# Low parts of weights, keys and activations: subtraction on VectorE in place of GpSimd

## The chip, the cores and the metric

The kernel runs on one core of a Trainium2 chip. The metric is the device time of one execution in microseconds. The engines are named as in the profile: PE is TensorE's matrix product and PEld its weight load, DVE is VectorE, ACT is ScalarE, POOL is GpSimd, SP issues transfers.

## What is computed

Causal attention by blocks of 64 on 4 batches, 8 heads, 576 positions, head size 64; then a two-layer block with squared ReLU; then a routed layer in which each of the 2304 tokens goes to one of 8 experts:

```python
attn_out = _attn_ref(q, k, v)                  # softmax(q k^T / 8, block-causal) v
x = attn_out.transpose(0, 2, 1, 3).reshape(B * S, H * D)      # 2304 x 512
r = np.maximum(x @ w_in, 0.0)                  # w_in 512 x 2048
x = (r * r) @ w_out                            # w_out 2048 x 512
logits = x @ w_gate + modality_bias[modality_id]
e_idx = np.argmax(logits, axis=1)
out[mask] = gate_w[mask, None] * (np.maximum(x[mask] @ w1[e], 0.0) @ w2[e])
```

## The kernel before

Matrix products run on fp32r operands. To keep precision, an operand is split in a high part, rounded to fp32r, and a low part, the difference; a product is then three products (high by high, high by low, low by high) into one PSUM bank. Names ending in `h` are high parts, those in `l` low parts. The rounding to the high part is a copy on ScalarE (or, for half of the expert weights, VectorE). The low part is one two-input subtraction.

The attention goes by batch, by chunks of 128 query rows (the fifth has 64), and by four pairs of heads (`attn_pair`). Keys are split once per head by `load_k`: L197 copies, L198 subtracts, on 64 of the 128 partitions. A K tile arrives in a raw buffer that is shared with the weights' pool `w`; only few of its buffers are free, so the next K load starts when L198 has read the one before. For the first batch the keys come in two parts, of 256 and 320 columns; for others in one of 576.

The weights of the first block are 64-bit words. `split_weight64` rebuilds a 32-bit float: L147 on ScalarE, three integer instructions on VectorE (L148, L149, L151), a copy on ScalarE (L153), and the subtraction L154. Sixteen pairs of 128x512 tiles are converted this way in the first part of the run, while the first two chunks of attention and the first block of tokens are computed. `split_weight` does the same for the two experts that get most tokens, for 32 tiles: every other tile (L164, L165) by ScalarE and GpSimd, the rest (L167, L168) by VectorE alone.

`ffn_units` computes 256 tokens at a time, in 16 units. A unit makes 12 products into `h` (L397 to L399), then r = relu(h) on ScalarE (L410), r*r (L411), the high part gh on ScalarE (L412), the low part gl (L413); the six products with the second weight (L387 to L389) follow after the next unit's first products. L411 runs on GpSimd in the first token block (`startup`) and on VectorE later. When a block is done, `route` computes the expert of each token and writes pairs to a list in DRAM by two indirect scatters from GpSimd (L494). Later GpSimd gathers rows (L547) and scatters results (L568).

The order on each engine is set by a scheduler that simulates the program while it is built; each engine then runs its instructions strictly in that order, waiting on semaphores. A changed engine for one instruction therefore changes the order of many others.

Of the kernel before, what the change touches and what calls it, by code (L numbers as in the profile page):

```python
# [10 lines left out]
F32 = mybir.dt.float32  # L11
# [9 lines left out]
P = 128  # L21
B, H, S, HD = 4, 8, 576, 64
# [28 lines left out]
def tile_attention_mlp_moe(ctx: ExitStack, tc: tile.TileContext, qT2, kT2, v, w_in, w_out,  # L51
                           mod, wg, bias, w1, w2, out):
    nc = tc.nc
# [9 lines left out]
    def pbank(tag, bufs):  # L63
        return ps.tile([P, 512], F32, tag=tag, bufs=BANKS[tag], name=tag)
# [63 lines left out]
    def wtile(dt):  # L128
        return wpool.tile([P, 2 * 512], dt, tag="w", bufs=2 * NF1 + 1, name="w")

    def parts_of(w):
        return w[:, 0:512], w[:, 512:1024]
# [7 lines left out]
    def split_weight64(raw):  # L140

        wh, wl = parts_of(wtile(F32R))
        wf = apool.tile([P, S], F32, tag="p", bufs=5, name="wf")[:, 0:512]
        wi = wf.bitcast(I32)
        words = raw.rearrange("p (f c) -> p f c", c=2)
        top, low = words[:, :, 1], words[:, :, 0]
        nc.scalar.activation(out=wf, in_=top.bitcast(F32), func=AF.Abs, scale=2.0 ** -112)  # L147
        nc.vector.tensor_scalar(wi, wi, 3, None, op0=ALU.logical_shift_left)  # L148
        nc.vector.scalar_tensor_tensor(out=wi, in0=top, scalar=-0x80000000, in1=wi, op0=ALU.bitwise_and,  # L149
                                       op1=ALU.bitwise_or)  # L150
        nc.vector.scalar_tensor_tensor(out=wi, in0=low, scalar=29, in1=wi, op0=ALU.logical_shift_right,  # L151
                                       op1=ALU.bitwise_or)
        nc.scalar.copy(wh, wf)  # L153
        nc.gpsimd.tensor_sub(wl, wf, wh.bitcast(F32))  # L154
        return wh, wl

    def split_weight(src):
        wh, wl = parts_of(wtile(F32R))
        raw = late.tile([P, 512], F32, tag="wraw", bufs=4, name="wraw")
        dst = raw.rearrange("p (k f) -> p k f", k=src.shape[1]) if len(src.shape) == 3 else raw  # L160
        nc.sync.dma_start(dst, src)
        nsplit[0] += 1
        if nsplit[0] % 2:
            nc.scalar.copy(wh, raw)  # L164
            nc.gpsimd.tensor_sub(wl, raw, wh.bitcast(F32))  # L165
        else:
            nc.vector.tensor_copy(wh, raw)  # L167
            nc.vector.tensor_sub(wl, raw, wh.bitcast(F32))  # L168
        return wh, wl
# [16 lines left out]
    def load_k(b, h, part=None):  # L186

        if part != 1:
            kst[b, h] = apool.tile([P, S], F32R, tag="ks", bufs=8, name=f"ks{b}_{h}")
        ks = kst[b, h]  # L190
        if part is None:
            raw = wtile(F32)[:, 0:S]
            nc.sync.dma_start(raw, kT2[b, h])
        else:
            raw = kpre[h][part]
            ks = (ks[:, 0:KS], ks[:, KS:S])[part]
        nc.scalar.copy(ks, raw)  # L197
        nc.gpsimd.tensor_sub(ks[HD:P], raw[HD:P], ks[HD:P].bitcast(F32))  # L198

    def load_v(b, hp, nk):  # L200
        vt = apool.tile([P, 5, P], F32, tag="v", bufs=2, name="v")
# [11 lines left out]
    startup = [True]  # L213
# [138 lines left out]
    def attn_units():  # L352

        res = []
        for b in range(B):
            for ci, (r0, nr) in enumerate(CHUNKS):
                for hp in range(H // 2):
                    def f(b=b, ci=ci, r0=r0, nr=nr, hp=hp):
                        if b == 0 and ci < 2:
                            load_k(b, 2 * hp, ci)  # L360
                            load_k(b, 2 * hp + 1, ci)
                        attn_pair(b, r0, nr, hp)
                        if ci == len(CHUNKS) - 1 and b < B - 1:
                            load_k(b + 1, 2 * hp)
                            load_k(b + 1, 2 * hp + 1)
                    nk = r0 + nr
                    cost = 2 * 2 * max(nk, 256) + 2 * nk * 3
                    res.append((b * S + r0, cost, f))
        return res


    def ffn_units(xh, xl, wa, wb, nf, square, finish, htag="h", bt=BT, last_blk=False):
        nt = -(-bt // P)
        acc = []
        pend = []

        def mm2(f, gh, gl):
            for t in range(nt):
                if f == 0:
                    acc.append(pbank("acc" if t < 2 else "h", 2))  # L380
                mm2t(f, t, gh, gl)

        def mm2t(f, t, gh, gl):
            wh, wl = wb[f]
            sl = slice(t * P, min((t + 1) * P, bt))
            n = sl.stop - sl.start
            nc.tensor.matmul(acc[t][:n], gh[:, sl], wh, start=(f == 0), stop=False)  # L387
            nc.tensor.matmul(acc[t][:n], gh[:, sl], wl, start=False, stop=False)  # L388
            return nc.tensor.matmul(acc[t][:n], gl[:, sl], wh, start=False, stop=(f == nf - 1))  # L389

        def unit(f):
            hb = pbank(htag, 2)
            wh, wl = wa[f]
            whk = wh.rearrange("p (k f) -> p k f", k=KC)
            wlk = wl.rearrange("p (k f) -> p k f", k=KC)
            for k in range(KC):
                nc.tensor.matmul(hb[:, :bt], whk[:, k, :], xh[:, k, :], start=(k == 0), stop=False)  # L397
                nc.tensor.matmul(hb[:, :bt], whk[:, k, :], xl[:, k, :], start=False, stop=False)  # L398
                nc.tensor.matmul(hb[:, :bt], wlk[:, k, :], xh[:, k, :], start=False, stop=(k == KC - 1))  # L399
            if last_blk:  # L400
                gh, gl = (x[:, :bt] for x in parts_of(wtile(F32R)))
            elif bt == BT:
                gh = work.tile([P, BT], F32R, tag="gh", bufs=3, name="gh")
                gl = work.tile([P, BT], F32R, tag="gl", bufs=3, name="gl")
            else:
                gh = late.tile([P, bt], F32R, tag="lgh", bufs=3, name="gh")
                gl = late.tile([P, bt], F32R, tag="lgl", bufs=3, name="gl")
            if square:
                r = work.tile([P, BT], F32, tag="r", bufs=2, name="r")
                nc.scalar.activation(out=r, in_=hb[:, :bt], func=AF.Relu)  # L410
                (nc.gpsimd if startup[0] else nc.vector).tensor_mul(r, r, r)  # L411
                nc.scalar.copy(gh, r)  # L412
                nc.gpsimd.tensor_sub(gl, r, gh.bitcast(F32))  # L413
            else:
                nc.scalar.activation(out=gh, in_=hb[:, :bt], func=AF.Relu)  # L415
                nc.vector.scalar_tensor_tensor(out=gl, in0=hb[:, :bt], scalar=0.0, in1=gh.bitcast(F32),  # L416
                                               op0=ALU.max, op1=ALU.subtract)
            pend.append((f, gh, gl))
            if len(pend) > 1 and not last_blk:
                mm2(*pend.pop(0))  # L420

        res = [lambda f=f: unit(f) for f in range(nf)]

        def last():
            if last_blk:
                for t in range(nt):
                    acc.append(pbank("acc", 2))
                    with tc.issue_after(mm.ins) if t else ExitStack():
                        for f, gh, gl in pend:
                            mm = mm2t(f, t, gh, gl)  # L430
                    finish(acc, t)
                return
            while pend:
                mm2(*pend.pop(0))
            for t in range(nt):
                finish(acc, t)
        res.append(last)
        return res
# [193 lines left out]
    def conv(f):  # L632
        if len(w_b) <= f < NF1:
            w_a.append(split_weight64(raws[2 * f]))
            w_b.append(split_weight64(raws[2 * f + 1]))
            if f + PRE < NF1:
                load_mlp(f + PRE)
# [21 lines left out]
    def expert_loads(i):  # L659
        wa, wb = [], []  # L660
        moe_w[i] = (wa, wb)

        def load(f):
            r = loads_reg(i)
            wa.append(split_weight(w1[ds(r, 1), :, f * P:(f + 1) * P].rearrange("o (k p) f -> p (o k) f", p=P)))
            wb.append(split_weight(w2[ds(r, 1), f * P:(f + 1) * P, :].rearrange("o p d -> p (o d)")))
        return [lambda f=f: load(f) for f in range(NF2)]
# [96 lines left out]
    with tc.If(njob > 0):  # L764
        with tc.For_i(0, E) as e:
            ne = nc.values_load(meta[0:1, ds(e, 1)], min_val=0, max_val=N // P)
            st = nc.values_load(meta[0:1, ds(e + E, 1)], min_val=0, max_val=CAP)
            with tc.If(ne > 0):
# [4 lines left out]
                with tc.For_i(0, ne) as c:  # L773
# [11 lines left out]
                    gh = gp.tile([P, FE], F32, name="ggh")  # L785
# [45 lines left out]
```

## Time and profile before

| what | value |
|---|---|
| median of three runs | 946.83 us (944.97 to 949.15) |
| profiled execution | 944.93 us |
| its span, first to last instruction | 943.0 us |
| mean granted TensorE clock | 0.975 |
| TensorE busy | 869.1 us (92%) |
| TensorE weight load | 742.4 us (79%) |
| VectorE busy | 516.6 us (55%) |
| ScalarE busy | 391.0 us (41%) |
| GpSimd busy | 314.2 us (33%) |

Shares are means over stages that differ: the attention and weight conversion at the start, the token blocks in the middle, the experts at the end. An instruction's duration in the trace includes the time in which it is held up after its start. Durations of VectorE instructions overlap a little with the next one's start, so what one takes out of the engine's time is the distance from start to start when it is fed without a break. PEclk is the granted share of TensorE's full clock.

### The profile page before, as it was taken

The numbers are of one execution on the slowest core, as the hardware profiler recorded it, in microseconds if no ns is written. First come the engines' busy times: TensorE is split into PE (matmuls) and PEld (weight loads), VectorE is DVE, ScalarE is ACT, GpSimd is POOL, SyncE is SP. The second block draws the span as 40 slices with busy tenths as digits, with TensorE's granted clock in tenths as the row PEclk, the third lists the DMA queues.
The fourth block names the chain that finished last, engine by engine and source line by source line (L and its number), as shares of the span: only waits on it lengthen the run. The fifth ranks groups of instructions, "written<-read, shape, count | busy, mean of one in ns | idle before, by whom it ended". The sixth has DMA issues, their size and how long they took to land. (4 is left out here: it accounts for less than half of the span.)

```text
span 943.0 us, 16448 instructions
## 1 busy us (share of the span) xinstructions
PE 869.1 (92%) x5961; PEld 742.4 (79%) x5962; DVE 516.6 (55%) x1411; ACT 391.0 (41%) x1076; POOL 314.2 (33%) x422
## 2 busy tenths in 40 slices
PE   5488878999989999989999999999898899999997
PEld 3266667788868888878888888888787688888896
DVE  5999997686637766536563664316622722122121
ACT  6566665555435544435443453334321312121111
POOL 3675766321333121234221221234612621021011
PEclk9689989999999999999999999999999999999999
DMA  9991114222133112034111111033303521010000
GB/s 315 286 321 48 48 40 116 79 48 79 53 91 100 60 43 57 26 90 114 49 29 40 41 51 38 26 80 108 84 23 77 187 65 42 20 58 31 12 28 36
DMA packets 87926, 73.98 MB, mean 78 GB/s; under 512 B 14305, under 2 KB 75745, under 8 KB 87842
## 3 DMA queue, kind: packets, MB, share of 16 engines
q1 hardware_dynamic: 84194, 63.18, 22.6%
q0 software_dynamic: 3648, 9.72, 3.3%
q8 instruction: 48, 0.79, 0.4%
q14 instruction: 36, 0.29, 0.1%
HBM read 62.71 MB, written 10.42 MB: 78 GB/s over the span
## 5 line engine op out<-in xcount | busy, mean ns | idle before, releaser
L413 POOL TENSOR_TENSOR gl<-r,gh 128x256 fp32r<-128x256 f32 x144 | 112.1, 779 | 284.9 <-ACT gh L412 197.0
L397 PE MATMUL h<-xh,w 128*128 128x256 f32 x576 | 169.8, 295 | 1.3 <-ACT w L153 1.3
L387 PE MATMUL acc<-w,gh 128*128 128x512 f32 x400 | 164.2, 411 | 3.7 <-ACT gh L412 2.9
L398 PE MATMUL h<-xl,w 128*128 128x256 f32 x576 | 164.8, 286 | 2.3 <-DVE xl L350 2.2
L399 PE MATMUL h<-xh,w 128*128 128x256 f32 x576 | 164.7, 286 | 1.4 <-POOL w L154 1.4
L388 PE MATMUL acc<-w,gh 128*128 128x512 f32 x400 | 158.5, 397 | 0.0
L389 PE MATMUL acc<-w,gl 128*128 128x512 f32 x400 | 143.4, 406 | 10.3 <-POOL gl L413 8.0
L397 PEld LDWEIGHTS h<-xh,w 128*128 128x128 f32 x576 | 110.7, 192 | 10.9 <-issue 3.8
L398 PEld LDWEIGHTS h<-xl,w 128*128 128x128 f32 x576 | 110.7, 192 | 6.5 <-DVE xl L350 2.5
L411 DVE TENSOR_TENSOR r<-r 128x256 f32<-128x256 f32 x128 | 64.3, 502 | 93.6 <-ACT r L410 93.4
L399 PEld LDWEIGHTS h<-xh,w 128*128 128x128 f32 x576 | 110.9, 193 | 2.3 <-POOL w L154 2.0
L410 ACT ACTIVATE r<-h 128x256 f32<-128x256 f32 x144 | 55.7, 386 | 119.7 <-PE h L399 117.3
L389 PEld LDWEIGHTS acc<-w,gl 128*128 128x128 f32 x400 | 72.7, 189 | 29.0 <-POOL gl L413 10.7
L416 DVE SCALAR_TENSOR_TENSOR gl<-pt,gh 128x352 fp32r<-128x352 f32 (+1 forms) x56 | 26.9, 480 | 124.8 <-ACT gh L415 124.8
L387 PEld LDWEIGHTS acc<-w,gh 128*128 128x128 f32 x400 | 76.2, 191 | 15.9 <-ACT gh L412 4.8
L412 ACT CAST gh<-r 128x256 fp32r<-128x256 f32 x144 | 58.5, 406 | 65.3 <-DVE r L411 65.0
L415 ACT ACTIVATE gh<-pt 128x352 fp32r<-128x352 f32 (+1 forms) x56 | 24.1, 430 | 144.2 <-PE pt L399 144.2
L388 PEld LDWEIGHTS acc<-w,gh 128*128 128x128 f32 x400 | 75.9, 190 | 9.2 <-POOL w L154 0.3
L397 PE MATMUL pt<-gxh,w 128*128 128x256 f32 (+1 forms) x256 | 78.5, 307 | 4.7 <-DVE gl L416 4.7
L399 PE MATMUL pt<-gxh,w 128*128 128x256 f32 (+1 forms) x256 | 77.7, 304 | 0.0
L398 PE MATMUL pt<-gxl,w 128*128 128x256 f32 (+1 forms) x256 | 77.6, 303 | 0.0
L286 ACT ACTIVATE p<-s,nmx 128x384 f32<-128x384 f32 (+2 forms) x96 | 56.5, 591 | 37.5 <-DVE nmx L281 17.3
(176 smaller groups left out, 1691.8 us busy)
## 6 DMA issues: line engine op xcount, KB each, us to landing
w<-w_in SPq DMA_DIRECT2D x16, 512.0 KB, 6.9
w<-w_out SPq DMA_DIRECT2D x16, 512.0 KB, 7.6
wraw<-w SPq DMA_DIRECT2D x32, 256.0 KB, 3.0
v<-v SPq DMA_DIRECT2D x28, 256.0 KB, 3.0
w<-kT SPq DMA_DIRECT2D x24, 288.0 KB, 2.9
qraw<-qT SPq DMA_DIRECT2D x48, 128.0 KB, 2.2
x2d<-x SPq DMA_DIRECT2D x18, 256.0 KB, 2.3
v<-v SPq DMA_DIRECT2D x12, 192.0 KB, 2.5
```

The costliest lines, as they stand in the source:

```text
L286: nc.scalar.activation(out=pb[:, c0:c0 + nv], in_=banks[i][:, :nv], func=AF.Exp, bias=nmx[:, 0:1], accum_out=sm[:, i:i + 1])
L387: nc.tensor.matmul(acc[t][:n], gh[:, sl], wh, start=(f == 0), stop=False)
L388: nc.tensor.matmul(acc[t][:n], gh[:, sl], wl, start=False, stop=False)
L389: return nc.tensor.matmul(acc[t][:n], gl[:, sl], wh, start=False, stop=(f == nf - 1))
L397: nc.tensor.matmul(hb[:, :bt], whk[:, k, :], xh[:, k, :], start=(k == 0), stop=False)
L398: nc.tensor.matmul(hb[:, :bt], whk[:, k, :], xl[:, k, :], start=False, stop=False)
L399: nc.tensor.matmul(hb[:, :bt], wlk[:, k, :], xh[:, k, :], start=False, stop=(k == KC - 1))
L410: nc.scalar.activation(out=r, in_=hb[:, :bt], func=AF.Relu)
L411: (nc.gpsimd if startup[0] else nc.vector).tensor_mul(r, r, r)
L412: nc.scalar.copy(gh, r)
L413: nc.gpsimd.tensor_sub(gl, r, gh.bitcast(F32))
L416: nc.vector.scalar_tensor_tensor(out=gl, in0=hb[:, :bt], scalar=0.0, in1=gh.bitcast(F32), op0=ALU.max, op1=ALU.subtract)
```

## The change

Five subtractions go from GpSimd to VectorE: L154 (low part of a first-block weight), L165 (of every other expert weight), L198 (of a key), L413 (of gl), and L411 (the square) in the first token block too. GpSimd keeps memsets, setup and the indirect transfers.

```diff
--- before.py
+++ after.py
@@ -151,7 +151,7 @@
         nc.vector.scalar_tensor_tensor(out=wi, in0=low, scalar=29, in1=wi, op0=ALU.logical_shift_right,
                                        op1=ALU.bitwise_or)
         nc.scalar.copy(wh, wf)
-        nc.gpsimd.tensor_sub(wl, wf, wh.bitcast(F32))
+        nc.vector.tensor_sub(wl, wf, wh.bitcast(F32))
         return wh, wl
 
     def split_weight(src):
@@ -162,7 +162,7 @@
         nsplit[0] += 1
         if nsplit[0] % 2:
             nc.scalar.copy(wh, raw)
-            nc.gpsimd.tensor_sub(wl, raw, wh.bitcast(F32))
+            nc.vector.tensor_sub(wl, raw, wh.bitcast(F32))
         else:
             nc.vector.tensor_copy(wh, raw)
             nc.vector.tensor_sub(wl, raw, wh.bitcast(F32))
@@ -195,7 +195,7 @@
             raw = kpre[h][part]
             ks = (ks[:, 0:KS], ks[:, KS:S])[part]
         nc.scalar.copy(ks, raw)
-        nc.gpsimd.tensor_sub(ks[HD:P], raw[HD:P], ks[HD:P].bitcast(F32))
+        nc.vector.tensor_sub(ks[HD:P], raw[HD:P], ks[HD:P].bitcast(F32))
 
     def load_v(b, hp, nk):
         vt = apool.tile([P, 5, P], F32, tag="v", bufs=2, name="v")
@@ -408,9 +408,9 @@
             if square:
                 r = work.tile([P, BT], F32, tag="r", bufs=2, name="r")
                 nc.scalar.activation(out=r, in_=hb[:, :bt], func=AF.Relu)
-                (nc.gpsimd if startup[0] else nc.vector).tensor_mul(r, r, r)
+                nc.vector.tensor_mul(r, r, r)
                 nc.scalar.copy(gh, r)
-                nc.gpsimd.tensor_sub(gl, r, gh.bitcast(F32))
+                nc.vector.tensor_sub(gl, r, gh.bitcast(F32))
             else:
                 nc.scalar.activation(out=gh, in_=hb[:, :bt], func=AF.Relu)
                 nc.vector.scalar_tensor_tensor(out=gl, in0=hb[:, :bt], scalar=0.0, in1=gh.bitcast(F32),
```

The scheduler's order shows the move at two places. The first is VectorE while weights are converted (wf is a weight being rebuilt, w its split tile, r and gl belong to a unit of the first token block). Before:

```order
L149 SCALAR_TENSOR_TENSOR wf_642<-w_166,wf_642 128x512
L148 TENSOR_SCALAR wf_650<-wf_650 128x512
L151 SCALAR_TENSOR_TENSOR wf_642<-w_166,wf_642 128x512
L149 SCALAR_TENSOR_TENSOR wf_650<-w_168,wf_650 128x512
L292 TENSOR_SCALAR sm_686<-sm_686 128x1
L292 TENSOR_SCALAR sm_704<-sm_704 128x1
L151 SCALAR_TENSOR_TENSOR wf_650<-w_168,wf_650 128x512
L293 RECIPROCAL sm_686<-sm_686 128x1
L293 RECIPROCAL sm_704<-sm_704 128x1
```

Now, at the conversion of the same tile (wf_650):

```order
L154 TENSOR_TENSOR w_578<-wf_579,w_578 128x512
L294 TENSOR_SCALAR p_596<-p_596,sm_595 128x384
L411 TENSOR_TENSOR r_676<-r_676 128x256
L294 TENSOR_SCALAR p_614<-p_614,sm_613 128x384
L149 SCALAR_TENSOR_TENSOR wf_650<-w_168,wf_650 128x512
L151 SCALAR_TENSOR_TENSOR wf_642<-w_166,wf_642 128x512
L292 TENSOR_SCALAR sm_686<-sm_686 128x1
L411 TENSOR_TENSOR r_765<-r_765 128x256
L413 TENSOR_TENSOR gl_675<-r_676,gh_674 128x256
L151 SCALAR_TENSOR_TENSOR wf_650<-w_168,wf_650 128x512
L313 MEMSET s_785 64x64
L292 TENSOR_SCALAR sm_704<-sm_704 128x1
```

Between the integer instructions now stand the subtraction of an earlier tile (w_578), two squares and a gl, which were in GpSimd's queue.

The second place is the change from the second batch to the third, with what each instruction waits for (DMASW is a transfer issued by GpSimd, DMAHW one issued by SP, ks a split key). On GpSimd before:

```order
L494 DMA lst_70<-pay_2925,pos_2944 22528x2 [waits DVE_49,Pool_49]
L413 TENSOR_TENSOR gl_3267<-r_3268,gh_3266 128x256 [waits Activation_49]
L494 DMA lst_70<-pay_2925,pos_2944 22528x2 [waits DMASW2_49]
L198 TENSOR_TENSOR ks2_2_3538<-w_3539,ks2_2_3538 64x576 [waits DMASW3_49,DMAHW7_49,Activation_49,Pool_49]
L413 TENSOR_TENSOR gl_3352<-r_3353,gh_3351 128x256 [waits Activation_49,Pool_49]
L198 TENSOR_TENSOR ks2_3_3543<-w_3544,ks2_3_3543 64x576 [waits DMAHW1_49,Activation_49,Pool_49]
```

On VectorE now, around the same gl_3352 and the same key ks2_2:

```order
L411 TENSOR_TENSOR r_3353<-r_3353 128x256 [waits Activation_49]
L281 TENSOR_REDUCE nmx_3494<-s_3497 128x1 [waits PE_49]
L281 TENSOR_REDUCE nmx_3494<-s_3502 128x1 [waits PE_49]
L247 SCALAR_TENSOR_TENSOR qlo_3724<-qraw_3718,qhi_3725 128x2x64 [waits DMAHW3_49,Activation_49,Pool_49]
L413 TENSOR_TENSOR gl_3352<-r_3353,gh_3351 128x256 [waits Activation_49]
L349 CAST xh3_2130<-pv_2994 128x64 [waits PE_49]
L220 COPY pt_3096<-pt_3097 128x512
L284 TENSOR_TENSOR nmx_3494<-nmx_3494 128x1 [waits DVE_49]
L350 TENSOR_TENSOR xl3_2131<-pv_2994,xh3_2130 128x64 [waits DVE_49]
L349 CAST xh4_3005<-pv_2994 128x64
L198 TENSOR_TENSOR ks2_2_3538<-w_3539,ks2_2_3538 64x576 [waits DMAHW6_49,Activation_49]
L350 TENSOR_TENSOR xl4_3006<-pv_2994,xh4_3005 128x64 [waits DVE_49]
```

The key's subtraction waited for the second scatter's landing (DMASW3) and gl_3352 stood behind it; now neither waits for a scatter, gl_3352 stands ahead of that key, and behind a reduction of scores that waits for PE.

## Rows read from the trace of the kernel before

**Rows 1.** Windows: length, busy us of PE, PEld, DVE, ACT, POOL, then clock, DMA.

```profile
20.00:150.00 130.00, 95.72 (x603) 73.22 (x604) 128.45 (x244) 83.09 (x211) 87.37 (x86) 0.88 0.47 150
180.00:620.00 440.00, 429.62 (x3263) 370.17 (x3261) 258.16 (x887) 205.80 (x605) 118.09 (x167) 0.99 0.21 58
260.00:280.00 20.00, 15.86 (x126) 13.36 (x125) 8.64 (x24) 6.38 (x16) 7.52 (x8) 0.91 0.27 74
620.00:760.00 140.00, 127.29 (x845) 110.73 (x841) 64.46 (x131) 40.68 (x96) 58.89 (x80) 0.99 0.32 94
```

**Rows 2.** Waits from 20 to 150 us: us in total, times, longest.

```profile
PE pt L301 <- DVE p L294: 9.4, 10, 2.8
```

**Rows 3.** Groups by shape, 20 to 150 us, DVE: busy us, mean ns, idle before.

```profile
L149 DVE SCALAR_TENSOR_TENSOR wf<-w,wf 128x512 int32<-128x512 int32 x32 | 30.8, 968 | 0.1
L151 DVE SCALAR_TENSOR_TENSOR wf<-w,wf 128x512 int32<-128x512 int32 x32 | 28.8, 902 | 0.0
L148 DVE TENSOR_SCALAR wf<-wf 128x512 int32<-128x512 int32 x32 | 25.8, 810 | 0.0
L294 DVE TENSOR_SCALAR p<-p,sm 128x512 f32<-128x512 f32 x8 | 7.7, 958 | 0.0
L268 DVE TENSOR_SCALAR p<-p,sm 128x256 f32<-128x256 f32 x8 | 5.8, 760 | 0.0
L247 DVE SCALAR_TENSOR_TENSOR qlo<-w,qhi 128x256 fp32r<-128x256 f32 x8 | 5.5, 692 | 0.0
```

**Rows 4.** Single lines over the whole span: min/median/max ns, first and last start.

```profile
L148 DVE TENSOR_SCALAR wf<-wf x32: 403/698/1650, 22.4 to 141.8; 128x512 int32<-128x512 int32 x32
...
L281 DVE TENSOR_REDUCE nmx<-s x96: 440/550/694, 43.5 to 586.9; 128x1 f32<-128x384 f32 x32, 128x1 f32<-128x512 f32 x32, 128x1 f32<-128x288 f32 x32
...
L247 DVE SCALAR_TENSOR_TENSOR qlo<-w,qhi x16: 396/414/1477, 6.2 to 92.4; 128x256 fp32r<-128x256 f32 x16
```

**Rows 5.** Timeline of DVE, 87 to 96 us: start us, us.

```profile
87.54 0.49 DVE L294 TENSOR_SCALAR p<-p,sm 128x512 f32<-128x512 f32 x1
...
94.68 0.41 DVE L148 TENSOR_SCALAR wf<-wf 128x512 int32<-128x512 int32 x1
95.01 0.67 DVE L151 SCALAR_TENSOR_TENSOR wf<-w,wf 128x512 int32<-128x512 int32 x1
95.61 0.41 DVE L148 TENSOR_SCALAR wf<-wf 128x512 int32<-128x512 int32 x1
```

**Rows 6.** Groups by shape, 20 to 150 us, POOL.

```profile
L154 POOL TENSOR_TENSOR w<-wf,w 128x512 fp32r<-128x512 f32 x31 | 44.7, 1449 | 36.6 <-ACT w L153 36.4
L413 POOL TENSOR_TENSOR gl<-r,gh 128x256 fp32r<-128x256 f32 x14 | 13.8, 988 | 4.4 <-ACT gh L412 4.3
L411 POOL TENSOR_TENSOR r<-r 128x256 f32<-128x256 f32 x15 | 12.5, 836 | 5.9 <-ACT r L410 5.9
L198 POOL TENSOR_TENSOR ks<-w,ks 64x320 fp32r<-64x320 f32 x8 | 9.0, 1150 | 0.2
```

**Rows 7.** Timeline of POOL before the two pauses, with the idle time before.

```profile
266.17 1.39 POOL L198 TENSOR_TENSOR ks<-w,ks 64x576 fp32r<-64x576 f32 x1 [2.77 <-DMA lst<-pay,pos]
267.64 0.72 POOL L413 TENSOR_TENSOR gl<-r,gh 128x256 fp32r<-128x256 f32 x1
...
411.66 1.39 POOL L198 TENSOR_TENSOR ks<-w,ks 64x576 fp32r<-64x576 f32 x1 [2.94 <-DMA lst<-pay,pos]
```

**Rows 8.** Timeline of PE at the two pauses.

```profile
268.41 0.80 PE L389 MATMUL acc<-w,gl 128*128 128x512 f32 x1 [4.14 <-POOL gl L413]
...
414.30 0.50 PE L389 MATMUL acc<-w,gl 128*128 128x512 f32 x1 [3.47 <-POOL gl L413]
```

**Rows 9.** Waits of PE from 180 to 620 us.

```profile
PE acc L389 <- POOL gl L413: 8.0, 3, 4.1
```

**Rows 10.** Groups by shape, 180 to 620 us, POOL.

```profile
L413 POOL TENSOR_TENSOR gl<-r,gh 128x256 fp32r<-128x256 f32 x101 | 74.8, 741 | 249.8 <-ACT gh L412 175.6 <-PE acc L389 66.0 <-PE acc L388 2.5
```

**Rows 11.** The page's second part: busy tenths of VectorE in 40 slices of the span.

```profile
DVE  5999997686637766536563664316622722122121
```

## The prediction

> **What bounds the kernel now.** I read the windows first, because the share over the whole span (VectorE 55%) hides the stages [rows 1]. From 20 to 150 us VectorE is busy 128.45 of 130 us and TensorE only 95.72: VectorE sets the pace there, and what TensorE waits for there is VectorE's work, such as the softmax scaling [rows 2]. From 180 to 620 us it is the other way round: TensorE is busy 429.6 of 440, VectorE 258.2. So a microsecond saved on VectorE before 150 us is a microsecond of the end; after 180 us only a pause of TensorE counts. The chain that ended last covers only the final expert blocks and says nothing of these stages.
>
> Second, how long one VectorE instruction takes. In the bound stretch the three integer instructions of a weight's conversion have means of 968, 902 and 810 ns, and the softmax scaling over 512 columns 958 [rows 3]. The same shapes can be much shorter: L148 ranges from 403 to 1650 ns, L247 from 396 to 1477, while L281, which reads PSUM alone, stays between 440 and 694 over three widths [rows 4]. The calm rows stand where GpSimd is idle, between 94.6 and 95.9 us: L148 0.41, L151 0.67; a calm L294 takes 0.49 [rows 5]. So a large part of VectorE's 128 us is not its own work but waiting for something that GpSimd's subtractions of the same stretch hold [rows 6].
>
> Third, TensorE's pauses in its own stage. The list of waits has one that matters: gl from GpSimd, 8.0 us in three waits [rows 9]. Up to 266 us GpSimd waits 2.77 us for the landing of an indirect scatter (L494) in front of a K subtraction (L198), and gl (L413) comes behind that; at 411 us it is 2.94 [rows 7]. TensorE stands still for 4.14 us, and for 3.47 the second time [rows 8]. The granted clock of 260 to 280 us is 0.91 of full speed [rows 1]: after the idle time, part of the stretch ran at the lower of the two levels, 1.2 GHz.
>
> **The change part by part.**
>
> *VectorE from 20 to 150 us, what it gains.* GpSimd keeps memsets and scatters, so no subtraction of it overlaps VectorE any more. Going back to calm durations gives [rows 3 to 5]: L149 32 x (0.968 - 0.67) = 9.5; L151 32 x (0.902 - 0.67) = 7.4; L148 32 x (0.810 - 0.41) = 12.8; L294 8 x (0.958 - 0.49) = 3.7; L268 8 x (0.760 - 0.35) = 3.3, its calm value put between L148's 0.41 and half of it plus a start; L247 8 x (0.692 - 0.41) = 2.2, calm value its median. Together 38.9 us. Smaller kinds stretch too and are not counted.
>
> *What it must do in addition* [rows 6]: 31 subtractions of 512 columns, 29 instructions of 256 columns (14 of L413, 15 of L411) and 8 of 320. Their slot is not the duration but the distance to the next start, since starts overlap: a two-input instruction of 512 columns occupies 0.60 us (95.01 to 95.61 in [rows 5]). I take 0.33 for 256 columns, a little over half, and 0.40 for 320. That is 18.6 + 9.6 + 3.2 = 31.4 us. Bounds of a 256-column slot: 0.30, half of 0.60, and 0.414, L247's median duration; the sum moves by -1 to +3.
>
> *Net in this stretch* -7.5 us, all of it on the path, since VectorE is what is short. If nothing were relieved it would be +31.4; if the uncounted kinds come too, perhaps -15, my estimate of twice the net. I take -7.5, since L148 shows both its values in one stretch and L281 does not [rows 4]. The Trainium skill, "SBUF — State Buffer", section "Who interferes with whom", would go further: VectorE's second SBUF port pair is GpSimd's only one and is held for a whole instruction, so a two-input or fast-mode instruction and a GpSimd one that reads SBUF exclude each other, and a reduction never contends. By it the relief is complete, uncounted kinds included, which is the -15 end; the spread of L148 and the narrow one of L281 agree with it.
>
> *The two pauses.* On VectorE neither gl nor the K subtraction waits for a scatter; the order shows a DMASW wait on L198 before and none now. The pauses of 4.14 and 3.47 us go, 7.6 us. Clock: 0.91 of 20 us [rows 1] is at most 1.8 us of full-speed work lost, and I take all of it; the second pause has the same shape, so 3.6 for both. Together -11.2. What is late next there: the raw K buffer is freed by L198 and the next K load starts then; it is freed earlier too, so nothing takes the pause's place at once.
>
> *VectorE from 180 to 620 us.* 101 of gl arrive [rows 10], 101 x 0.33 = 33 us, and 16 K subtractions of 576 columns at 0.67 = 11, in a stage where VectorE has 182 us free; its own stretched instructions give some back. At nothing, apart from lateness: VectorE is in order, and gl now waits behind a reduction (up to 0.69 [rows 4]) or a scaling, and everything behind gl waits for ScalarE's gh. The cover is the unit's lag: TensorE takes gl only after the next unit's first product, and of 101 only three made TensorE wait, two of them by the scatter [rows 9]. With gl itself shorter (0.42, as L247's median, for 0.74) I put +2 us, between 0 and the price of rival B.
>
> *620 to 760 us.* The 16 subtractions of expert weights add 16 x 0.60 = 9.6 to 64.5 busy of 140 [rows 1], so 75 us free cover them: nothing; without that cover, 9.6. After 760 us the change touches nothing. Before 20 us eight K subtractions of 256 columns come to VectorE, 8 x 0.33 = 2.6 us, while it is about half busy (the first digit of its line in [rows 11]): nothing.
>
> *Sum:* -7.5 - 11.2 + 2 = -16.7 us. The profiled execution took 944.93 us, a span of 943.0 and 1.9 around it; the sum gives 928.2 for it. It is 1.9 us faster than the median of the three runs, 946.83, and since a median is to be forecast I take 946.83 - 16.7 = **930 us**.
>
> **The rivals.**
>
> *A. VectorE is full, so it gets longer.* If the stretch came from elsewhere, 31.4 us would be added before 150 us and only the pauses would go: 946.8 + 31.4 - 11.2 = 967. For it: 99% busy. Against it: calm rows of 0.41 beside 1650 ns of the same instruction, and reductions that never stretch. 0.08. The Trainium skill, "Perfetto Trace Analysis", section "Optimizing Scalar/DVE Operations", speaks for this side: with a saturated VectorE, work may be moved to ScalarE or even GpSimd, which is the reverse of this change; but it adds that the shared port may eat such a gain.
>
> *B. gl late in TensorE's stage (the slower side).* Each unit's chain now passes VectorE twice (L411, L413) behind attention's work, 101 times. If a unit loses 0.4 us, it costs 40 us: 970. It decides at the point where VectorE's backlog exceeds the lag of about a microsecond that the few waits of [rows 9] show; losing 0.17 us a unit takes the whole gain back. For it: VectorE would go from 59% to as much as 69% busy (258.2 + 33 + 11 of 440), and the order is new everywhere. Against: only three waits of 101 with a GpSimd instruction that is longer. 0.06 for over 951.6, 0.07 for about no change.
>
> *C. The relief comes but the first stage is then held by something else*, the loads or the round trip from ScalarE to VectorE and back; only the pauses go, with 2 us of new waits: 946.8 - 9.2 = 938. 0.17.
>
> *D. It does not do what it says.* The order has no L154, L165, L198, L411 or L413 on GpSimd; no chance left for it.
>
> **How the numbers follow.** About 0.5% (4.7 us) is what a measurement of this kernel can tell from no change. The forecast has 0.62, C 0.17, both faster than 942.1; B near zero 0.07, B slower 0.06, A 0.08. That is 0.79 faster, 0.07 same, 0.14 slower. The range: below, the first stage at -15, the pauses at -11.2, and a third of the 15.6 us that the clock of 0.88 in 130 us stands for [rows 1], -5: 915. Above, it takes in C and the milder B: 948. A and the worse B stay out.
>
> **What would show it.** VectorE: L148 near 0.41, L149 and L151 near 0.68 in all 32; 20 to 150 us shorter by some 7 us, with VectorE still nearly full. The pauses behind gl at two scatters gone from TensorE's waits; gl waits on VectorE few and under 1 us. Wrong if L148 stays at 0.8 (A), if the list of waits shows TensorE behind gl from VectorE for tens of microseconds (B), or if VectorE is no longer full before 150 us while TensorE gains nothing (C).

## The result, and the profile after

The changed kernel takes **918.66 us** (median of 4 runs, 917.86 to 919.97), beside 947.18 us before (4 runs): a ratio of 0.9692, 95% interval 0.9669 to 0.9714. The profiled execution took 919.97 us against 944.93, with a span of 918.2 against 943.0. The forecast was 930, with a range of 915 to 948.

The page's first two parts (busy time of each engine; VectorE's busy tenths in 40 slices, as in [rows 11]):

```profile
PE 865.1 (94%) x5961; PEld 743.7 (81%) x5962; DVE 535.9 (58%) x1659; ACT 392.3 (43%) x1076; POOL 81.6 (9%) x174
...
DVE  7999997867667765666663865338332722122211
```

VectorE's busy time rose by only 19.3 us (from 516.6), although 248 more instructions came to it. The windows, two of them moved 20 us forward because the work came forward (to be set against [rows 1]; length, busy time of PE, PEld, DVE, ACT, POOL, then clock, DMA share, GB/s):

```profile
20.00:150.00 130.00, 107.03 (x698) 84.53 (x699) 126.08 (x341) 92.33 (x239) 12.78 (x16) 0.87 0.53 165
180.00:600.00 420.00, 416.02 (x3197) 358.43 (x3196) 269.08 (x941) 196.68 (x571) 21.07 (x51) 1.00 0.23 59
260.00:280.00 20.00, 19.31 (x183) 16.92 (x181) 12.55 (x41) 10.67 (x30) 0.59 (x3) 1.00 0.50 137
600.00:740.00 140.00, 127.79 (x826) 113.28 (x826) 67.81 (x171) 41.50 (x97) 21.13 (x42) 0.96 0.33 95
```

In the first 130 us TensorE does 107.03 us of work instead of 95.72, VectorE executes 341 instructions instead of 244, and it is still all but full. In the middle TensorE now lacks 4.0 of 420 us; before it lacked 10.4 of 440.

VectorE's groups by shape from 20 us to the end of the first token block (148.2 us), those that answer to [rows 3] and those that came from [rows 6] (busy us, mean ns | idle before):

```profile
L154 DVE TENSOR_TENSOR w<-wf,w 128x512 fp32r<-128x512 f32 x32 | 21.7, 682 | 0.4 <-ACT w L153 0.3
L151 DVE SCALAR_TENSOR_TENSOR wf<-w,wf 128x512 int32<-128x512 int32 x32 | 21.5, 678 | 0.0
L149 DVE SCALAR_TENSOR_TENSOR wf<-w,wf 128x512 int32<-128x512 int32 x32 | 21.5, 678 | 0.1
L148 DVE TENSOR_SCALAR wf<-wf 128x512 int32<-128x512 int32 x32 | 12.9, 417 | 0.4 <-ACT wf L147 0.3
L411 DVE TENSOR_TENSOR r<-r 128x256 f32<-128x256 f32 x17 | 7.0, 412 | 0.9 <-ACT r L410 0.9
L413 DVE TENSOR_TENSOR gl<-r,gh 128x256 fp32r<-128x256 f32 x16 | 6.6, 411 | 0.0
...
L294 DVE TENSOR_SCALAR p<-p,sm 128x512 f32<-128x512 f32 x8 | 3.8, 474 | 0.0
L198 DVE TENSOR_TENSOR ks<-w,ks 64x576 fp32r<-64x576 f32 x5 | 3.8, 756 | 0.2
L198 DVE TENSOR_TENSOR ks<-w,ks 64x320 fp32r<-64x320 f32 x8 | 3.6, 488 | 0.1
...
L247 DVE SCALAR_TENSOR_TENSOR qlo<-w,qhi 128x256 fp32r<-128x256 f32 x8 | 3.2, 408 | 0.0
...
L268 DVE TENSOR_SCALAR p<-p,sm 128x256 f32<-128x256 f32 x7 | 2.1, 341 | 0.0
```

L148 went from 810 to 417, L149 from 968 to 678. There is no second value left: all 32 of L148 lie between 398 and 497 ns, where they reached 1650 before [rows 4]:

```profile
L148 DVE TENSOR_SCALAR wf<-wf x32: 398/414/497, 20.7 to 130.1; 128x512 int32<-128x512 int32 x32
```

TensorE's waits in its own stage, 180 to 600 us (total, times, longest; compare [rows 9]):

```profile
PE pt L301 <- ACT pt L218: 2.5, 2, 1.7
...
PE acc L389 <- DVE gl L413: 0.2, 1, 0.2
```

The 8.0 us behind gl are 0.2 us now. In place of the second pause one of 1.75 us is left near 400 us, without a scatter in front of it (VectorE, then SP, ScalarE and TensorE):

```profile
395.34 0.76 DVE L198 TENSOR_TENSOR ks<-w,ks 64x576 fp32r<-64x576 f32 x1 [2.37 <-ACT ks L197]
...
396.13 0.34 SPq L193 DMA_DIRECT2D w<-kT  x1
...
398.91 0.67 ACT L197 CAST ks<-w 128x576 fp32r<-128x576 f32 x1 [2.97 <-DMA w<-kT]
399.49 0.58 ACT L218 COPY pt<-pt 128x512 f32<-128x512 f32 x1
...
400.12 0.33 PE L301 MATMUL pt<-ident,p 128*128 128x128 f32 x1 [1.75 <-ACT pt L218]
```

When L198 has read one key's raw tile (396.10), the next key's transfer is issued; ScalarE's copy L197 of that key waits 2.97 us for the data, and L218, which TensorE needs, stands behind it. The granted clock from 400 to 420 us is 0.91, as it was from 410 to 430 us before: part of the stretch still runs at the lower level, 1.2 GHz, after the pause.

One pause is new, in the timeline of TensorE behind the first gather of expert rows, where before the same wait was 1.42 us:

```profile
656.88 1.12 PE L553 MATMUL s<-ident,gat 128*128 128x128 f32 x4 [6.25 <-DMA gat<-x2d,il]
```

Where the 24.8 us of the span came from, stage by stage, is best read from four events: VectorE's copy at the end of a token block (the starts of L679), and the start of the third transfer of expert rows (L568). All kernels of this study are in one table, as us against the profiled run of before, where these starts stand at 161.88, 316.17, 589.71 and 763.40 us:

| kernel | block 0 | block 2 | block 6 | third L568 | span |
|---|---|---|---|---|---|
| the change | -13.7 | -23.2 | -23.3 | -24.8 | 918.2 |
| L154 alone moved | -10.0 | -16.5 | -15.3 | -10.9 | 932.2 |
| L198 alone moved | -2.4 | -12.9 | -14.1 | -10.7 | 931.9 |
| L411, L413 alone moved | -2.3 | -2.4 | -1.4 | +4.8 | 947.4 |
| L165 alone moved | -1.8 | -1.5 | -2.3 | -3.8 | 939.2 |
| the change, L154 back | -4.8 | -14.9 | -17.0 | -19.6 | 923.1 |
| the change, L198 back | -8.4 | -11.1 | -9.4 | -11.4 | 931.6 |
| the change and added subtractions | +13.3 | +2.6 | +2.5 | 0.0 | 942.8 |
| the change and added fills | -1.2 | -14.1 | -15.6 | -17.6 | 925.4 |
| the change, first-stage scaling and squares on ScalarE | -20.2 | -31.2 | -31.6 | -33.2 | 909.8 |
| the change, gathers later | -12.9 | -23.4 | -24.7 | -27.1 | 915.9 |
| both | -21.3 | -33.5 | -33.3 | -36.3 | 907.0 |

Each row is one execution; its time lies up to 3.7 us from the median of its kernel (L411, L413 alone: 949.19 against 945.50).

So the change gave 13.7 us in the first stage, 9.6 between blocks 0 and 6, and about 1.5 after that. Between the ends of blocks 0 and 6 TensorE was idle for 4.0 us instead of 11.5.

### The profile page after: what moved, and what is told of

It is laid out like the page before. It is cut to its first block, busy times and chain, and to the rows that moved or that the text cites. A ratio compares the mean times of both kernels' runs of the same rounds, so it can differ in the third digit from the quotient of the medians.

```text
span 918.2 us, 16334 instructions
## 1 busy us (share of the span) xinstructions
PE 865.1 (94%) x5961; PEld 743.7 (81%) x5962; DVE 535.9 (58%) x1659; ACT 392.3 (43%) x1076; POOL 81.6 (9%) x174
## 5 line engine op out<-in xcount | busy, mean ns | idle before, releaser
L397 PE MATMUL h<-xh,w 128*128 128x256 f32 x576 | 172.7, 300 | 2.1 <-ACT r L410 1.4
L399 PE MATMUL h<-xh,w 128*128 128x256 f32 x576 | 165.8, 288 | 2.2 <-DVE w L154 2.2
L411 DVE TENSOR_TENSOR r<-r 128x256 f32<-128x256 f32 x144 | 60.7, 421 | 66.7 <-ACT r L410 65.6
L415 ACT ACTIVATE gh<-pt 128x352 fp32r<-128x352 f32 (+1 forms) x56 | 24.1, 429 | 139.7 <-PE pt L399 137.3
L413 DVE TENSOR_TENSOR gl<-r,gh 128x256 fp32r<-128x256 f32 x144 | 60.5, 420 | 30.9 <-ACT gh L412 29.5
L286 ACT ACTIVATE p<-s,nmx 128x384 f32<-128x384 f32 (+2 forms) x96 | 56.4, 590 | 29.2 <-DVE nmx L281 8.3
```

The lines of the kernel that those rows point to most:

```text
L286: nc.scalar.activation(out=pb[:, c0:c0 + nv], in_=banks[i][:, :nv], func=AF.Exp, bias=nmx[:, 0:1], accum_out=sm[:, i:i + 1])
L411: nc.vector.tensor_mul(r, r, r)
L413: nc.vector.tensor_sub(gl, r, gh.bitcast(F32))
```

## The experiments

Theory one is the prediction's: GpSimd's subtractions hold up VectorE's instructions, VectorE bounds the start, and two pauses of TensorE vanish. Theory two is that the start gains because the low half of a weight is ready sooner (0.68 us in place of 1.45). Theory three is that the middle gains because g's low half is. (g is the squared hidden layer of a unit, made by L411 to L413; "the keys" stands for L198, "the start" for the time to the end of block 0, "the middle" for that from block 0 to block 6.)

### One part of the change alone, and one part put back

Each of these has one engine name different. **L154 alone** (before, plus):

```diff
-        nc.gpsimd.tensor_sub(wl, wf, wh.bitcast(F32))
+        nc.vector.tensor_sub(wl, wf, wh.bitcast(F32))
```

> Only L154, the low half of a converted weight, goes to VectorE; L198, L411 and L413 stay on GpSimd. Theory one (GpSimd's subtractions stretch VectorE, and VectorE bounds the start): L154 was 44.9 of the 80.4 us that GpSimd's four kinds took in 20 to 150 us, so the start loses its share of the stretch, some 28 us, against 31 x 0.68 = 21 us added: block 0 ends about 7 us sooner, and the two TensorE pauses of 4.1 and 3.5 us behind L413 stay; about 940 us. L148 falls from 0.70 to about 0.55 at its median, not to 0.41. Theory two (the start gains because the low half of a weight is ready sooner, 0.68 us in place of 1.45): all of the start's 13.7 us come here, about 933 us.

Measured: 932.97 us, ratio 0.9867 (0.9834 to 0.9900). The time is the one theory two gave, but the stages are not: the start gains 10.0 us, more than the 7 of theory one and less than the 13.7 of theory two, and the middle gains 5.3, where theory one expected both pauses to stay. Only the second did (4.15 us behind gl, at 399.5); at the first no pause of TensorE over 1.2 us is left, though a key waited for the scatter there as before (3.00 us). Which change of order did that stays open. L148's median fell to 0.415 us at once (0.55 was expected); single ones still reach 1.08. **The reverse** (the changed kernel with L154 back on GpSimd):

> The changed kernel with L154 alone back on GpSimd (L165, L198, L411 and L413 stay on VectorE). Theory one: the start loses L154's share again, about 7 us, and the middle keeps its gain: about 926 us; L148, L149 and L151 stretch again beside L154 only. Theory two: all of the start's 13.7 us are lost, about 932 us.

Measured: 925.43 us, ratio 0.9794 (0.9763 to 0.9826), as theory one had it; the start loses 8.9 us of its 13.7. L148 and L151 reach 1.47 and 1.75 us again; L149, against the expectation, stays under 0.70. L154 alone, the keys alone and g alone gain 10.0, 2.4 and 2.3 us there, which is 14.7 against 13.7 for all. Theory two can't say why the keys and g gain anything at the start, where their own instructions are added to a full VectorE.

**L198 alone** (the key's low part on VectorE):

```diff
-        nc.gpsimd.tensor_sub(ks[HD:P], raw[HD:P], ks[HD:P].bitcast(F32))
+        nc.vector.tensor_sub(ks[HD:P], raw[HD:P], ks[HD:P].bitcast(F32))
```

> Only L198, the low part of a key tile, goes to VectorE. Theory one: L198 was 9.2 of 80.4 us of GpSimd's work in the start, so the start gains about 2 us; the g subtraction L413 no longer stands behind a queued L198 on GpSimd, so both pauses go, 8 to 10 us in the middle stages: about 936 us. Theory three (the middle gains because g's low half is ready sooner on VectorE): the pauses are worth little by themselves, about 945 us.

**L411 and L413 alone** (square and low part of g on VectorE):

```diff
-                (nc.gpsimd if startup[0] else nc.vector).tensor_mul(r, r, r)
+                nc.vector.tensor_mul(r, r, r)
...
-                nc.gpsimd.tensor_sub(gl, r, gh.bitcast(F32))
+                nc.vector.tensor_sub(gl, r, gh.bitcast(F32))
```

> Only L411 and L413, square and low half of g, go to VectorE. Theory one: L411 and L413 were 26.3 of 80.4 us of GpSimd's work in the start, worth 16.6 us of stretch against 29 x 0.41 = 12 us added, so block 0 ends about 5 us sooner; the pauses go as well, 8 to 10 us, since g no longer stands on GpSimd: about 932 us. Theory two: nothing at the start, about 937 us. Theory three: the middle's whole 10.5 us here and none with the keys alone, about 932 to 937 us.

Measured: the keys alone 933.06 us, ratio 0.9862 (0.9820 to 0.9904); g alone 945.50 us, ratio 1.0001 (0.9978 to 1.0024). Theory three is refuted, and so is my forecast for g alone: with g's subtraction on VectorE, 11.1 us of pauses are there all the same, behind ScalarE. TensorE's waits from 180 to 620 us with g alone moved:

```profile
PE pt L301 <- ACT pt L218: 6.1, 2, 4.8
PE h L397 <- ACT r L410: 5.0, 3, 3.2
```

and with the keys alone moved, where gl is still made by GpSimd:

```profile
PE pt L301 <- ACT pt L218: 1.7, 1, 1.7
PE acc L389 <- POOL gl L413: 1.2, 2, 0.9
```

What ScalarE waited for shows when the timelines of POOL, SP and ACT with g alone moved are laid side by side (start, duration, idle before):

```profile
266.71 1.40 POOL L198 TENSOR_TENSOR ks<-w,ks 64x576 fp32r<-64x576 f32 x1 [3.04 <-issue]
...
268.13 0.34 SPq L193 DMA_DIRECT2D w<-kT  x1
...
270.98 0.67 ACT L197 CAST ks<-w 128x576 fp32r<-128x576 f32 x1 [5.91 <-DMA w<-kT]
271.55 0.38 ACT L410 ACTIVATE r<-h 128x256 f32<-128x256 f32 x1
```

The key's subtraction, held behind a scatter's wait, ends at 268.11. At 268.13 the next key's transfer is issued, since only then is its raw tile free. The copy L197 of that key waits for the data until 270.98, and ScalarE's relu, which TensorE needs, stands behind it in order. In the kernel before it was the same: L198 ends at 413.05 [rows 7], and the transfer and the copy follow:

```profile
413.07 0.34 SPq L193 DMA_DIRECT2D w<-kT  x1
...
416.09 0.67 ACT L197 CAST ks<-w 128x576 fp32r<-128x576 f32 x1 [6.99 <-DMA w<-kT]
```

So gl from GpSimd was only the wait that came last (with L154 alone moved, the held key by itself did not stop TensorE at the first scatter). To see whether the key alone brings the pauses back, **the changed kernel with L198 back on GpSimd**:

> The changed kernel with L198 alone back on GpSimd. Theory (the subtraction of a key tile stands behind a scatter's wait on GpSimd, holds the tile that the next key's load needs, and ScalarE stands behind that load): TensorE's pauses of 3 to 5 us come back, once between the ends of blocks 1 and 2 and once near 400 us, though g's own subtraction is on VectorE; 8 to 10 us in the middle and 2.4 us at the start: about 930 us. Rival (the pauses need g on GpSimd behind the key's subtraction): the middle stays and only the start loses 2.4 us: about 921 us.

Measured: 936.16 us, ratio 0.9921 (0.9895 to 0.9947). Its three events again, the second time:

```profile
400.73 1.39 POOL L198 TENSOR_TENSOR ks<-w,ks 64x576 fp32r<-64x576 f32 x1 [3.14 <-issue]
...
402.15 0.34 SPq L193 DMA_DIRECT2D w<-kT  x1
...
405.13 0.67 ACT L197 CAST ks<-w 128x576 fp32r<-128x576 f32 x1 [9.30 <-DMA w<-kT]
```

TensorE's pause behind it is 5.25 us, and 2.66 us at the first scatter, with nothing of g on GpSimd. Between the ends of blocks 0 and 6 this kernel gains 1.0 us where the changed kernel gains 9.6: 8.6 us lost, as the theory said. The start lost 5.3 us and not 2.4, about half of the 6 us by which the time exceeds what was expected. The trace shows where: VectorE gives up 7.4 us of key subtractions, yet until the end of block 0 it is busy 128.9 us instead of 124.7, since its other instructions stretch again (means of 759 ns instead of 682 for L154, 642 instead of 341 for L268 over 256 columns, 533 instead of 412 for L411).

**L165 alone** (every other expert weight):

```diff
-            nc.gpsimd.tensor_sub(wl, raw, wh.bitcast(F32))
+            nc.vector.tensor_sub(wl, raw, wh.bitcast(F32))
```

> Only L165, the low half of every second expert weight tile, goes to VectorE. Prediction's step (the end of the program, 620 to 760 us, gains nothing): within 1.5 us of the kernel before. Rival (the end gains by L165 alone): from the second to the third write of expert rows took 23.5 us before, and in the kernels with the keys, the conversion or g alone 23.5, 28.4 and 29.3 us, but 20.1 and 19.3 us in the changed kernel and the one with L154 back, which are those with L165 on VectorE; then that stretch is near 20 us here and the end comes some 4 us sooner, about 942 us. Block 0 to block 6 end where they ended before.

Measured: 942.81 us, ratio 0.9986 (0.9967 to 1.0004): by the times nothing that can be told from no change. In the profile the third L568 comes 19.2 us after the second instead of 23.5, as the rival said, but block 8 ends 1.7 us later than before; its wait for the first gather is 3.23 us instead of 1.42. With L154 or g alone moved the same stretch took 28.5 and 29.3 us; why it grew there, no run shows.

### GpSimd's work added back, with and without reading

In both, GpSimd gets work behind each of the 32 weight tiles; nothing reads its result, and VectorE keeps all that the change gave it. The scratch tile is held about as long in both (1.81 us for a subtraction, 3 x 0.59 for the fills). The first adds a subtraction:

```diff
-        nc.vector.tensor_sub(wl, wf, wh.bitcast(F32))
+        nc.vector.tensor_sub(wl, wf, wh.bitcast(F32)); nc.gpsimd.tensor_sub(wf, wh.bitcast(F32), wl.bitcast(F32))
```

> The changed kernel, with an idle subtraction added on GpSimd behind each of the 32 weight tiles (wh minus wl into the scratch tile that is free by then, 128 x 512, two operands read; nothing reads the result). Theory one (GpSimd's subtractions stretch VectorE): putting L154 back cost 8.8 us at block 0's end although it took 32 x 0.68 = 21.8 us off VectorE, so 32 such subtractions stretch it by some 30 us; here nothing is taken off, so block 0 ends 20 to 30 us later than in the changed kernel, and L148, L149 and L151 show single instructions of 1.3 us and more again; about 940 to 948 us. Theory two (the gain came from when wl is ready, or from the order of the instructions): VectorE makes wl as in the changed kernel and nobody waits for the addition, so within 4 us of 918.7 us.

The second adds fills:

```diff
-        nc.vector.tensor_sub(wl, wf, wh.bitcast(F32))
+        nc.vector.tensor_sub(wl, wf, wh.bitcast(F32)); [nc.gpsimd.memset(wf, 0.0) for _ in range(3)]
```

> The same with three fills of the scratch tile on GpSimd (128 x 512 each, nothing read) in place of the subtraction: some 1.5 us of GpSimd per weight tile, held as long. Theory one: a fill does not stretch VectorE as a subtraction does, so L148, L149 and L151 stay at 0.41 and 0.68 us at their longest 0.75, and the time is within 4 us of 918.7 us. If any GpSimd work stretches VectorE, or holding the scratch tile 1.5 us longer is what costs, this comes out as late as the kernel with the added subtraction.

Measured: with subtractions 943.82 us, ratio 0.9972 (0.9956 to 0.9989), block 0 ends 27.0 us later than in the changed kernel. With fills 928.63 us, ratio 0.9829 (0.9806 to 0.9852), block 0 ends 12.5 us later. Single instructions of VectorE from 20 to 150 us (min/median/max ns), with subtractions:

```profile
L148 DVE TENSOR_SCALAR wf<-wf x30: 397/415/1493, 20.7 to 147.9; 128x512 int32<-128x512 int32 x30
...
L149 DVE SCALAR_TENSOR_TENSOR wf<-w,wf x29: 669/679/1754, 21.6 to 147.3; 128x512 int32<-128x512 int32 x29
```

and with fills:

```profile
L148 DVE TENSOR_SCALAR wf<-wf x32: 402/414/822, 21.2 to 142.4; 128x512 int32<-128x512 int32 x32
...
L149 DVE SCALAR_TENSOR_TENSOR wf<-w,wf x32: 661/676/693, 22.1 to 146.1; 128x512 int32<-128x512 int32 x32
```

The subtraction stretches both kinds, as theory one says: VectorE is busy 126.73 of the 130 us there, as in the changed kernel (126.08), but gets through 281 instructions instead of 341. Until the end of block 0 its busy time rises by 26.8 us (151.5 against 124.7) and its idle time by 0.2, so the 27.0 us are longer instructions and not the wait for the scratch tile. Theory two, which has this kernel near 918.7, is refuted. With fills, L149, which reads two SBUF tiles, stays at its calm 0.69 us or less, but L148, which reads one tile and a constant, reaches 0.82. My "a fill does not stretch VectorE" was thus wrong for half of the kinds. The softmax scaling, also one tile and a factor, shows it in the groups by shape of the same kernel:

```profile
L148 DVE TENSOR_SCALAR wf<-wf 128x512 int32<-128x512 int32 x32 | 15.1, 480 | 0.1
...
L294 DVE TENSOR_SCALAR p<-p,sm 128x384 f32<-128x384 f32 x8 | 6.3, 790 | 0.1
```

Against 417 and 399 ns that is 32 x 0.063 + 8 x 0.391 = 5.1 us; the other widths of L294 and L268 bring it to 7.3 us of the 12.5. Another 3.0 us are instructions that came into the longer time before the end of block 0, and VectorE's idle time rose by 2.2 us. ScalarE waited 11.6 us for the scratch tile that the fills held (L286 7.2, L147 4.4; with the subtractions 24.1), which may be the reason for the idle time; no run separates it. The Trainium skill, "SBUF — State Buffer", section "Who interferes with whom", says both halves: an instruction of VectorE with two inputs in SBUF contends only with a GpSimd instruction that reads SBUF, and one of the kind of `tensor_scalar`, when it runs in a mode that takes both ports, with any. The rows of both kernels agree with it (L149 at most 0.69 us beside fills and 1.75 beside subtractions, L148 0.82 beside fills), though no row names the mode.

The stretch can be summed for every kernel: from 20 us to the end of block 0, each duration on VectorE minus the median of its shape in the changed kernel, over all shapes (us).

| kernel | stretch | of L154, L198, L411, L413 on GpSimd |
|---|---|---|
| before | 48.1 | all |
| L165 alone moved | 47.6 | all |
| L411, L413 alone moved | 37.1 | L154, L198 |
| L198 alone moved | 36.5 | L154, L411, L413 |
| L154 alone moved | 19.6 | L198, L411, L413 |
| the change, L154 back | 25.2 | L154 |
| the change, L198 back | 12.5 | L198 |
| the change and added subtractions | 27.2 | none, but 32 added subtractions |
| the change and added fills | 7.3 | none, but 96 added fills |

In the changed kernel the sum is nil; each part left on GpSimd or put back there brings some of it.

### What is left at the start

From 20 to 130 us of the changed kernel VectorE is busy 108.0 of 110 us and ScalarE 78.1. So in the first stage the softmax scalings and squares were put on ScalarE:

```diff
+                if startup[0]:
+                    nc.scalar.mul(pb[:, j, :nk], pb[:, j, :nk], sm[:, 2 + j:3 + j])
+                else:
+                    nc.vector.tensor_scalar_mul(pb[:, j, :nk], pb[:, j, :nk], sm[:, 2 + j:3 + j])
...
+                if startup[0]:
+                    nc.scalar.activation(out=r, in_=r, func=AF.Square)
+                else:
+                    nc.vector.tensor_mul(r, r, r)
```

(L294 in the same way.)

> The changed kernel, with the softmax scalings L268 and L294 and the squares L411 of the first stage on ScalarE. Theory one (VectorE, 108.0 of 110 us busy between 20 and 130 us, still bounds the start): 8 x 0.47 + 7 x 0.34 + 17 x 0.41 = 13 us leave it, and ScalarE has 32 of those 110 us free, so block 0 ends 5 to 13 us sooner: about 910 us. Rival (once the stretch is gone, the chains through ScalarE and TensorE set the start): no gain, 916 to 922 us.

Measured: 908.90 us, ratio 0.9601 (0.9578 to 0.9624); block 0 ends 6.5 us sooner than in the changed kernel. VectorE still sets the start of the changed kernel, so that work taken off it is a gain. The Trainium skill, "Perfetto Trace Analysis", section "Optimizing Scalar/DVE Operations", says that with a saturated VectorE it may make sense to move work to ScalarE, or even to GpSimd, but that the port shared by GpSimd and VectorE may leave no gain in the second case. For ScalarE this run agrees (908.9 against 918.7 us); for GpSimd the run with L154 put back shows the warning at work (925.4 against 918.7).

The new pause at the first gather was tried by giving out the gathers two units later in the program:

```diff
-        if f == NF1 // 2 + 2:
+        if f == NF1 // 2 + 4:
```

> The changed kernel, with the first gathers of the experts two units later in the last block's loop. If the 6.25 us that TensorE waits at 650.6 us for the gathered rows is an order that puts the transposes ahead of the data, it shrinks to under 2 us and the end comes 4 us sooner: about 914.5 us. If the rows are only late with respect to the lists, the pause moves to the next step that needs them, and the time stays within 2 us of 918.7 us.

Measured: 916.22 us, ratio 0.9685 (0.9666 to 0.9703). The end comes 2.4 us sooner in the profiled run, but not by what was expected: the pause is 6.07 us still, and it begins as long after the end of block 7 as in the changed kernel (30.8 us in both): the edit did not move the transposes away from it. Both edits together:

> The changed kernel with both: the first stage's softmax scalings and squares on ScalarE (8.5 us sooner at the end of the profiled run than the changed kernel) and the first gathers emitted two units later (2.4 us sooner). If the two are apart in time and add: about 907 us. If the later gathers were worth nothing by themselves: 909 us.

Measured: **907.14 us**, ratio 0.9603 (0.9584 to 0.9622), faster than both kernels, but by its ratio no better than the first edit alone (0.9601). The later gathers are not shown to be worth anything.

## Why the prediction was right, and which term was off

The direction, the two stages and the mechanism of the first stage held; that of the pauses held in part. The gain was 25.0 us between the profiled executions (28.5 between the medians) where 16.7 was forecast: 13.7 in the first stage for 7.5, 9.6 between blocks 0 and 6 for 9.2, and 1.5 after that for nothing. So most of what was missing is in the first stage. By its steps:

**The calm durations** gave 38.9 us for six kinds. By the means of the changed kernel they gave 9.3 + 7.2 + 12.6 + 3.9 + 3.4 + 2.3 = 38.7 us (L149, L151, L148, L294, L268, L247). This step was right to about one per cent, because the calm rows were in the trace of before.

**"Smaller kinds stretch too and are not counted"** is the step that was mis-sized. From 20 us to the end of block 0 the kernel before has these rows, which no group of the prediction held (by shape: busy us, mean ns):

```profile
L294 DVE TENSOR_SCALAR p<-p,sm 128x384 f32<-128x384 f32 x8 | 4.7, 593 | 0.0
...
L247 DVE SCALAR_TENSOR_TENSOR qlo<-qraw,qhi 128x256 fp32r<-128x256 f32 x4 | 3.1, 768 | 0.9 <-ACT qhi L246 0.8
...
L247 DVE SCALAR_TENSOR_TENSOR qlo<-qraw,qhi 128x128 fp32r<-128x128 f32 x4 | 2.9, 731 | 0.0
...
L284 DVE TENSOR_TENSOR nmx<-nmx 128x1 f32<-128x1 f32 x4 | 2.3, 580 | 0.0
L289 DVE SCALAR_TENSOR_TENSOR sm<-sm 128x1 f32<-128x1 f32 x4 | 2.3, 563 | 0.5 <-ACT p L286 0.5
```

and the changed kernel these:

```profile
L294 DVE TENSOR_SCALAR p<-p,sm 128x384 f32<-128x384 f32 x8 | 3.2, 399 | 0.0
...
L247 DVE SCALAR_TENSOR_TENSOR qlo<-qraw,qhi 128x256 fp32r<-128x256 f32 x4 | 1.6, 408 | 0.0
...
L247 DVE SCALAR_TENSOR_TENSOR qlo<-qraw,qhi 128x128 fp32r<-128x128 f32 x4 | 1.1, 274 | 0.0
...
L289 DVE SCALAR_TENSOR_TENSOR sm<-sm 128x1 f32<-128x1 f32 x4 | 0.6, 154 | 0.4 <-ACT p L286 0.4
L284 DVE TENSOR_TENSOR nmx<-nmx 128x1 f32<-128x1 f32 x4 | 0.6, 145 | 0.0
```

That is 1.6 + 1.4 + 1.8 + 1.7 + 1.6 = 8.1 us, and 9.6 with L265 and the widest L294: the whole relief is 48.3 us.

**What VectorE must do in addition** was put at 31.4 us. With the prediction's slots and the counts of the profile after (32 x 0.60, 33 x 0.33, 8 x 0.40, and five K subtractions of 576 columns that came into the stretch, 5 x 0.67) it is 36.7. Then 48.3 - 36.7 = 11.6 us less work for VectorE, where the windows show 11.9 (136.60 to 124.67). The end of the block came 13.7 us sooner, the other 1.8 being idle time of VectorE (5.3 to 3.5). The net was to be -7.5, with an end of -15 for complete relief; the measured 13.7 lies near that end.

**The two pauses** (11.2 us with the clock). The gain of 9.6 us in the middle is near the forecast 9.2 (11.2 less 2 for late gl), and in part that is luck. The two pauses behind gl are gone, but the prediction had nothing take their place, and 1.75 us near 400 us did; and of the two stretches at the lower clock one stayed, so that half of the 3.6 us for the clock did not come. TensorE's short waits elsewhere in the middle, which the prediction did not count, fell from 3.9 us to 2.2. The cause was named only in part. The prediction put the pause down to gl queued behind the key's subtraction. It did say that the raw K buffer is freed by L198 and the next K load starts then, but took that for a thing that might come next, while it was the heart of it: g alone gave nothing in the middle (0.9 us lost), the keys alone took 11.7 us off it. The sum was right because the change moves both; by the same reasoning g alone was forecast to end the pauses, and it did not.

**+2 us for late gl** (and rival B behind it): 0.2 us in one wait. VectorE's backlog in the middle exceeded the unit's lag once.

**"620 to 760 us: nothing"** came out so by two things that cancel. L165 on VectorE shortens the way to the third L568 (19.2 against 23.5 us with it alone), and the wait for the first gather grows from 1.4 to 6.25 us. That pause was not foreseen, and its cause is open. It is not that TensorE arrives sooner: with the added subtractions block 7 ends 1.8 us later than before, and the pause is 6.38 us. The first gather itself starts 33.7 us after the end of block 7 instead of 29.6. The pause is 1.4 and 1.5 us with L154 or the keys alone moved, 2.9 with g alone and 3.2 with L165 alone, 4.87 with the key back and 6.1 with L154 back: it grows with the parts on VectorE that run in that stretch, g and L165.

**Rivals.** A (VectorE fuller by 31.4 us) is refuted by the mean of L148, B by the waits, C by block 0, which ended 13.7 us sooner.

## What to carry to other kernels

Where VectorE is full and GpSimd computes beside it, look for one shape with two durations: the shorter, from moments when GpSimd is idle, prices what moving GpSimd's work over gives back, and it should be summed over all kinds, down to the 128x1 ones. Of a pause that the trace puts down to one late operand, ask what else the held engine holds: here an operand's buffer, its next transfer, and a third engine that stood in order behind that. Move one part at a time, since the part named in the wait was worth nothing by itself.

## What was not expected of the hardware

A fill by GpSimd, which reads nothing, still held up VectorE's instructions with one tile and a factor (L294 over 384 columns: 790 ns for 399; L148 up to 822), while L149, with two tiles, kept 661 to 693 ns. And instructions of 128x1 elements with two inputs took 563 to 580 ns beside GpSimd's subtractions against 145 to 154 alone: even the smallest instruction pays the wait.
